# Value product of a windowed attention: from one 128-row product per unit to two 64-row products by halves of the keys

## The chip, the cores and the metric

The program runs on one core of a Trainium2 chip. The metric is device time in microseconds (us) of one execution, as the median of several runs. Engines are called PE (TensorE matmul), PEld (TensorE weight load), DVE (VectorE), ACT (ScalarE), POOL (GpSimd) and SP (SyncE, which only issues DMAs here).

## What is computed

A token-wise gate mixes an attention block and a gated linear unit over one sequence of 2048 tokens of width 512, all in float32:

```
g = sigmoid((x * gate_w).sum(-1, keepdims=True))
# a: 32 heads of width 16, causal, each query sees the last 256 keys
qkv = x @ wqkv
scores = einsum("bhqd,bhkd->bhqk", q, k) * 16 ** -0.5, masked to 0 <= i - j < 256
a = (softmax(scores) @ v) @ wo
# b: F = 1376
b = (sigmoid(x @ w_gate) * (x @ w_up)) @ w_down
out = g * a + (1 - g) * b
```

## The kernel before

**Stages.** A first stage (to about 38 us of the span) loads and splits x and the first weights and makes V and the first projections. Large products run in the reduced float32 type with each operand split into a high and a low part, so that a product over 512 inputs takes 12 matmuls (4 blocks of 128 inputs, 3 pairs of parts). The second stage, to about 560 us, is a loop over u (L766). The last stage makes the two output projections and the mix.

**Units.** The attention is cut into 128 units: 8 groups of 4 heads times 16 blocks of 128 tokens. Unit w needs three steps, which the loop does at different u: `s_part` (L305) at u = w makes the scores of a query block against its keys and DVE takes their maximum (L321); `st_part` (L353) at u = w + 9 (`LAG`) makes the scores again with keys on the rows and ACT takes the exponential into the tile `pt` (L366), which POOL masks (L368); the value product at u = w + 11 (`PVLAG`) multiplies `pt` (128 keys by up to 3 x 128 queries) with the values of 4 heads and adds to the PSUM tile `pv` (L394). A key block serves 3 query blocks (2 and 1 at the end of a group), 45 blocks of 128 columns in 16 units. `pv` is one bank of 4 query blocks used as a ring, so the product is cut in two where it wraps (6 of 16 units).

**Array halves.** The score matmuls have 64 rows: head hh uses rows 0 to 63 or 64 to 127 by hh % 2 (`blk`, L298). All work that fills the loop, the projections of queries and keys (`pj`), of the gated unit (`gu`) and its tail (`tp`), is also done with 64 rows at a time: `group_mm` (L242) takes half of the rows of a block. A generator `turns` (L632) hands this work out: one turn is one matmul of 512 columns on the lower half (half 0) and one on the upper (half 1), of different output tiles. Three groups of 12 steps go through each half in different orders (`TURN`), the upper half 6 turns behind (`SHIFT`), so that the second half of a group starts 6 turns after its first half ended and adds to the same PSUM tile. `turns` yields after 3 turns (`GAP`).

**Order of a unit.** PE, ACT, SP and DVE follow the order in which the loop is written. For u from 9 to 127 the loop does, for each of 4 heads, one `s` matmul on one half and one `st` matmul on the other, and then 3 turns (none after the last head of odd u), so 21 turns in two units. At the start of every even u it does the value products of two units as one burst: for each query range 4 matmuls of 128 rows by 32 columns, one for each head, beside each other in the array. After a burst `o_take` copies the two finished query blocks from `pv` (L410, ACT, 256 columns) and DVE clears them (L411). Copies out of PSUM at the end of a group wait in a list `acts` and are emitted one at each head; `behind` is the same for DVE. PSUM has two tiles each for `s` and `st`, three for `misc` (pj, gu, tp) and one for `pv`.

Of the kernel before, what the change touches and what calls it, by code (L numbers as in the profile page):

```python
# [10 lines left out]
AF = mybir.ActivationFunctionType  # L11
# [9 lines left out]
HG = 4  # L21
# [19 lines left out]
SD = 3  # L41
QB = 32
HOLD = 3
GAP = 3
SHIFT = 6
TURN = ((0, 2, 1), (1, 0, 2))
TAIL = 109
# [9 lines left out]
def gated_mix_kernel(  # L57
# [71 lines left out]
    with ExitStack() as actx:  # L129
# [112 lines left out]
        def group_mm(pt, wh, wl, c, k, half, second):  # L242
            d, w = divmod(k, 2) if k < 2 * ND else (k - 2 * ND, 2)
            r = slice(0, P) if half is None else slice(64 * half, 64 * half + 64)
            mm(pt, (wl if w == 2 else wh)[r, d], (xl if w == 1 else xh)[r, d, c * CH:(c + 1) * CH],  # L245
               start=k == 0 and not second, stop=k == 3 * ND - 1 and (half is None or second),
               skip_group_check=half is not None)

        def proj_mm(s, k, half=None, second=False):
            g, c = divmod(s, NC)  # L250
            if s not in pj:
                pj[s] = ps.tile([P, CH], F32, tag="misc", name=f"pj{s}", bufs=3)
            group_mm(pj[s], *wq[g], c, k, half, second)

        def proj_raw(s):
            raws[s] = cpool.tile([P, CH], F32, tag="sp", name=f"pr{s}", bufs=4)
# [48 lines left out]
        def s_part(u, hh):  # L305
            g, i = divmod(u, NB)
            s = g * NC + i // 4
            if i % 4 == 0 and hh == 0:
                mxs[s] = spool.tile([P, HG, 4], F32, tag="mx", name=f"mx{s}")
            k0 = max(0, i - 2)  # L310
            tag = "st" if u < LAG and hh >= 2 else "s"
            pt = ps.tile([P, 3 * P], F32, tag=tag, name=f"s{u}_{hh}", bufs=2)
            lhsT = blk(g, i, hh, 0)
            for k, e in pieces(g, k0, i + 1):
                mm(  # L315
                    pt[:, (k - k0) * P:(e - k0) * P], lhsT, blk(g, k, hh, 1, e - k),
                    start=k == k0, stop=e == i + 1, skip_group_check=True,
                )
            n = (i + 1 - k0) * P
            junk = spool.tile([P, 3 * P], F32, tag="junk", name=f"junk{u}_{hh}", bufs=1)  # L320
            nc.vector.tensor_tensor_reduce(  # L321
                junk[:, 0:n], pt[:, 0:n], mask[:, 3 * P - n:], scale=1.0, scalar=NEG,
                op0=ALU.add, op1=ALU.max, accum_out=mxs[s][:, hh, i % 4:i % 4 + 1],
            )
# [24 lines left out]
            )  # L349

        pts = {}

        def st_part(u, hh):  # L353
            g, j = divmod(u, NB)
            if u not in pts:
                pts[u] = ppool.tile([P, HG, 3 * P], F32, tag="pt", name=f"pt{u}", bufs=3)
            pt = ps.tile([P, 3 * P], F32, tag="st", name=f"st{u}_{hh}", bufs=2)
            lhsT = blk(g, j, hh, 1)
            last = min(NB, j + 3)
            for q, e in pieces(g, j, last):  # L360
                mm(  # L361
                    pt[:, (q - j) * P:(e - j) * P], lhsT, blk(g, q, hh, 0, e - q),
                    start=q == j, stop=e == last, skip_group_check=True,
                )
            n = (last - j) * P
            nc.scalar.activation(pts[u][:, hh, 0:n], pt[:, 0:n], AF.Exp, scale=SCALE)  # L366

        def mask_p(u):  # L368
            j = u % NB
# [12 lines left out]
        acts = []  # L382
        obs = {}

        def pv_part(u):
            g, j = divmod(u, NB)
            p = pts.pop(u)
            last = min(NB, j + 3)
            q = j
            while q < last:  # L390
                e = min(last, (q // 4 + 1) * 4)
                for hh in range(HG):
                    h = g * HG + hh
                    mm(  # L394
                        pv[32 * hh:32 * hh + 32, (q % 4) * P:(q % 4 + e - q) * P],
                        V[:, j, h * VW:h * VW + 32],
                        p[:, hh, (q - j) * P:(e - j) * P],
                        start=False, stop=True, skip_group_check=True,
                        tile_position=(0, 32 * hh),
                    )  # L400
# [4 lines left out]
        def o_take(s, half):  # L405
            g, c = divmod(s, NC)
# [3 lines left out]
            nc.scalar.copy(obs[s][:, cols], pv[:, cols])  # L410
            behind.insert(0, lambda: nc.vector.memset(pv[:, cols], 0.0))  # L411
            if half == 0:
# [79 lines left out]
        def gu_mm(f, c, w, k, half=None, second=False):  # L492
            if (f, c, w) not in gp:
                gp[f, c, w] = ps.tile([P, CH], F32, tag="misc", name=f"gu{f}_{c}_{w}", bufs=3)
            group_mm(gp[f, c, w], gv[:, 0, w], gv[:, 1, w], c, k, half, second)

        def gu_post(f, c, w):
            t = cpool.tile([P, CH], F32, tag="sp", name=f"sp{f}_{c}_{w}", bufs=4)
# [35 lines left out]
        def tail_mm(b, k, half=None, second=False):  # L534
            if b not in tp:
                tp[b] = ps.tile([P, CH], F32, tag="misc", name=f"tp{b}", bufs=3)
            d, w = divmod(k, 3)
            r = slice(0, P) if half is None else slice(64 * half, 64 * half + 64)
            mm(tp[b][:, 0:TW], (xl if w == 1 else xh)[r, d, b * P:(b + 1) * P], tw[d][int(w == 2)][r, 0:TW],  # L539
               start=k == 0 and not second, stop=k == 3 * ND - 1 and (half is None or second),  # L540
               skip_group_check=half is not None)

# [89 lines left out]
        def turns():  # L632
            k3 = 3 * ND
            groups = []
            halves_done = {}
            for t in range(n_rest * k3 + SHIFT):
                if t and t % GAP == 0:
                    yield
                if t % (3 * k3) == 0 and len(groups) < n_rest:
                    groups.extend((work or rest).pop(0) for _ in range(3))  # L640
                for half, v in enumerate((t, t - SHIFT)):
                    if 0 <= v < n_rest * k3:
                        n, k = divmod(v, k3)
                        n += TURN[half][n % 3] - n % 3
                        groups[n][0](k, half, n in halves_done)
                        if k == k3 - 1:
                            halves_done[n] = halves_done.get(n, 0) + 1
                            if halves_done[n] == 2:
                                _, after, post = groups[n]
                                if after is None:  # L650
                                    post()
                                else:
                                    acts.insert(0, lambda after=after, post=post: (post(), after()))

        def slot(h, d, c):
            return (xh, xl)[h][:, d, c * CH:(c + 1) * CH]
# [109 lines left out]
        for u in range(N):  # L766
# [42 lines left out]
            for hh in range(HG):  # L809
                if hh == 0 and u % 2 == 0:  # L810
                    for w in (u - PVLAG - 1, u - PVLAG):
                        if 0 <= w < NU:
                            pv_part(w)
                if u < NU:
                    s_part(u, hh)
                if 0 <= u - LAG < NU:
                    st_part(u - LAG, hh ^ 1 if u < NU else hh)
                if u < LAG:
# [5 lines left out]
                else:  # L824
                    if behind:
                        behind.pop(0)()
                    if acts and (u < NU or hh % 2 == 1):
                        acts.pop(0)()
                if u >= LAG and (hh < HG - 1 or u % 2 == 0 if u < NU else hh % 2 == 1):
                    next(slots, None)  # L830
                    if u >= NU and not (hh == HG - 1 and u % 2 == 1 and u > NU + 1):
                        next(slots, None)
            if u < LAG:
                flush(soon)
# [192 lines left out]
```

## Time and profile before

| | before |
|---|---|
| median of 3 runs | 738.04 us (737.7 to 738.16) |
| the profiled execution | 737.77 us |
| its span, first to last instruction | 736.1 us |
| granted TensorE clock over the span | 1.00 |
| PE busy | 730.0 us (99%) |
| DVE, ACT, POOL busy | 507.1 us, 430.4 us, 170.7 us |

The profile is that of one execution, so sums are made against 737.77 us, 1.7 us of which lie outside the span. Starts of matmuls are recorded and their ends are modelled, so that durations overlap: what an instruction takes is read from start to start. In a row of the timeline, "64\*128" after the tiles' names is the part of the array that a matmul uses, rows by columns; "64x384" is its moving operand, and "x4" merges neighbours of one kind into a row.

### The profile page before, as it was taken

The page shows a single profiled execution, that of the slowest core. Times are in us where ns is not written, and L with a number is a line of the kernel's source. Part 1 is how long each engine was busy: PE and PEld are TensorE (multiplying, and loading weights), DVE is VectorE, ACT ScalarE, POOL GpSimd, SP SyncE. Part 2 cuts the span into 40 slices and gives each one's busy share as a digit, 9 for nine tenths or more (in the row PEclk, how much of TensorE's full clock was granted, in tenths as well). Part 3 has the DMA queues.
Part 4 walks back from the last instruction along what each step waited for, and adds up shares of the span by engine and source line. Part 5 has one row for each costly group of instructions (what it writes and reads, how often), then busy time and mean ns, then how long its engine had stood idle before and what let it go on. Part 6 is the DMA issues. An engine that isn't in the chain of part 4 may idle for free.

```text
span 736.1 us, 17727 instructions
## 1 busy us (share of the span) xinstructions
PE 730.0 (99%) x6298; PEld 578.3 (79%) x6298; DVE 507.1 (69%) x1519; ACT 430.4 (58%) x922; POOL 170.7 (23%) x256
## 2 busy tenths in 40 slices
PE   9999999999999999999999999999999999999997
PEld 7888777887777878778777777778887888787886
DVE  5378867667776776776777677678846877658481
ACT  6423666576666666756757667676566654534341
POOL 5200333233233232323323323323341000000000
PEclk9999999999999999999999999999999999999999
DMA  8441334534445353452534524544477867878431
GB/s 300 108 116 43 102 106 120 152 88 127 129 116 142 86 153 109 123 156 59 165 106 107 152 76 128 160 135 152 154 233 190 281 173 175 224 172 252 131 74 57
DMA packets 94464, 103.65 MB, mean 141 GB/s; under 512 B 44942, under 2 KB 57486, under 8 KB 94376
## 3 DMA queue, kind: packets, MB, share of 16 engines
q1 hardware_dynamic: 94376, 102.53, 50.0%
q8 instruction: 49, 0.80, 0.5%
q14 instruction: 39, 0.32, 0.1%
HBM read 45.32 MB, written 31.99 MB: 105 GB/s over the span
## 4 chain that ended last, share of the span: by engine, by line
PE 97%; DVE 1%; DMA 1%; issue 1%; ACT 0%; SPq 0%; DVEq 0%
PE gu L245 28%; PE pv L394 12%; PE pj L245 11%; PE s L315 7%; PE st L361 5%; PE tp L539 5%; PE pd L79 5%; PE pd L81 5%; PE pd L80 5%; PE vh L576 3%; PE pa L79 2%; PE pa L80 2%; PE pa L81 2%; PE vps L440 1%; DVE junk L321 1%; DMA V<-in_wv_dram 1%
## 5 line engine op out<-in xcount | busy, mean ns | idle before, releaser
L321 DVE CUSTOM_DVE_ANT_0 junk<-s,mask 128x384 f32<-128x384 f32 (+2 forms) x512 | 271.6, 530 | 123.4 <-PE s L315 57.3
L366 ACT ACTIVATE pt<-st 128x384 f32<-128x384 f32 (+2 forms) x512 | 241.1, 475 | 166.0 <-PE st L361 66.6
L245 PE MATMUL gu<-xh,w 64*128 64x512 f32 x1152 | 271.1, 393 | 0.0
L245 PE MATMUL gu<-xl,w 64*128 64x512 f32 x576 | 183.0, 392 | 0.0
L371 POOL TENSOR_SCALAR_AFFINE_SELECT pt<-pt 128x512 f32<-128x512 f32 x128 | 86.5, 675 | 373.2 <-ACT pt L366 369.6
L361 PE MATMUL st<-ring 64*128 64x384 f32 (+2 forms) x536 | 168.1, 331 | 0.0
L315 PE MATMUL s<-ring 64*128 64x384 f32 (+2 forms) x536 | 166.7, 329 | 0.7 <-DVE mx L321 0.7
L245 PEld LDWEIGHTS gu<-xh,w 64*128 64x128 f32 x1152 | 150.9, 185 | 13.7
L315 PEld LDWEIGHTS s<-ring 64*128 64x128 f32 x536 | 95.3, 184 | 39.8 <-DVE nm L332 8.1
L361 PEld LDWEIGHTS st<-ring 64*128 64x128 f32 x536 | 96.3, 184 | 10.3 <-issue 2.7
L394 PE MATMUL pv<-pt,V 128*32 128x384 f32 (+2 forms) x1408 | 91.0, 388 | 0.0
L245 PEld LDWEIGHTS gu<-xl,w 64*128 64x128 f32 x576 | 87.7, 185 | 4.0
L245 PE MATMUL pj<-xl,wqh 64*128 64x512 f32 (+1 forms) x228 | 80.0, 392 | 0.0
L245 PE MATMUL pj<-xh,wqh 64*128 64x512 f32 (+1 forms) x228 | 79.8, 392 | 0.0
L376 POOL TENSOR_SCALAR_AFFINE_SELECT pt<-pt 128x512 f32<-128x512 f32 x112 | 74.8, 668 | 0.0
L245 PE MATMUL pj<-xh,wql 64*128 64x512 f32 (+1 forms) x228 | 69.8, 391 | 0.0
L394 PEld LDWEIGHTS pv<-pt,V 128*32 128x32 f32 x1408 | 37.2, 109 | 35.1 <-issue 28.8
L79 PE MATMUL pd<-ring,hb 128*128 128x512 f32 x160 | 63.1, 395 | 0.0
L81 PE MATMUL pd<-ring,hb 128*128 128x512 f32 x160 | 62.8, 393 | 0.0
L80 PE MATMUL pd<-ring,hb 128*128 128x512 f32 x160 | 62.1, 388 | 0.0
L75 ACT CAST hb<-V 128x512 fp32r<-128x512 f32 x40 | 24.9, 622 | 61.7 <-DVE V L730 47.7
L245 PEld LDWEIGHTS pj<-xh,wql 64*128 64x128 f32 (+1 forms) x228 | 41.2, 185 | 3.1
(129 smaller groups left out, 1133.1 us busy)
## 6 DMA issues: line engine op xcount, KB each, us to landing
gu_scratch<-sp SPq DMA_DIRECT2D x72, 256.0 KB
V<-gu_scratch SPq DMA_DIRECT2D x36, 512.0 KB
ring<-sh SPq DMA_DIRECT2D x128, 128.0 KB
ring<-sl SPq DMA_DIRECT2D x64, 128.0 KB
guraw<-in_wgu_dram SPq DMA_DIRECT2D x18, 256.0 KB
oT_scratch<-ob SPq DMA_DIRECT2D x128, 32.0 KB
xl<-oT_scratch SPq DMA_DIRECT2D x16, 256.0 KB
out_dram<-spare SPq DMA_DIRECT2D x16, 256.0 KB
```

What stands on the lines that cost most here:

```text
L79: mm(ps, lh, rh, start=first, stop=False)
L80: mm(ps, lh, rl, start=False, stop=False)
L81: mm(ps, ll, rh, start=False, stop=last)
L245: mm(pt, (wl if w == 2 else wh)[r, d], (xl if w == 1 else xh)[r, d, c * CH:(c + 1) * CH], start=k == 0 and not second, stop=k == 3 * ND - ...
L315: mm(pt[:, (k - k0) * P:(e - k0) * P], lhsT, blk(g, k, hh, 1, e - k), start=k == k0, stop=e == i + 1, skip_group_check=True,)
L321: nc.vector.tensor_tensor_reduce(junk[:, 0:n], pt[:, 0:n], mask[:, 3 * P - n:], scale=1.0, scalar=NEG, op0=ALU.add, op1=ALU.max, accum_out ...
L361: mm(pt[:, (q - j) * P:(e - j) * P], lhsT, blk(g, q, hh, 0, e - q), start=q == j, stop=e == last, skip_group_check=True,)
L366: nc.scalar.activation(pts[u][:, hh, 0:n], pt[:, 0:n], AF.Exp, scale=SCALE)
L371: nc.gpsimd.affine_select(p[:, :, 0:P], p[:, :, 0:P], pattern=[[0, HG], [1, P]], compare_op=ALU.is_ge, fill=0.0, base=0, channel_multiplie ...
L376: nc.gpsimd.affine_select(p[:, :, 2 * P:], p[:, :, 2 * P:], pattern=[[0, HG], [-1, P]], compare_op=ALU.is_gt, fill=0.0, base=0, channel_mu ...
L394: mm(pv[32 * hh:32 * hh + 32, (q % 4) * P:(q % 4 + e - q) * P], V[:, j, h * VW:h * VW + 32], p[:, hh, (q - j) * P:(e - j) * P], start=Fals ...
L539: mm(tp[b][:, 0:TW], (xl if w == 1 else xh)[r, d, b * P:(b + 1) * P], tw[d][int(w == 2)][r, 0:TW], start=k == 0 and not second, stop=k == ...
```

## The change

- The value product of a unit is divided by keys: `pv_quads(w, 0)` takes keys 0 to 63 on the lower half of the array and `pv_quads(w, 1)` keys 64 to 127 on the upper half, each with 4 matmuls of 64 rows by 32 columns for a query range. The last two units keep 128 rows.
- A unit has two bursts in place of four pairs. In burst 0 the value product on the lower half is written beside the four score matmuls (`s` and `st` of heads 1 and 3) of the upper half, in burst 1 the other way round. Where the product is cut in two, the second part is written after the first score matmul. Behind each burst stand 5 turns (6 behind burst 1 of odd u).
- Each unit's finished query block is copied and cleared by itself, 128 columns a unit, right after its second burst; the two value products of a unit follow each other by one burst, and the next unit's first product needs the cleared tile.
- Explicit dependencies (`after`): the first value matmul of each half waits for the last exponential emitted so far, and the first matmul of the second half of a group for the first exponential emitted after its first half.
- Copies at the end of a group are emitted in `turns` itself, not by way of `acts`.

```diff
-GAP = 3
+    def after(ins, other):
+        tc.add_manual_dep(
+            ins.ins, other.ins.name,
+            mybir.DependencyInfo(mybir.DependencyClass.Sync, mybir.DependencyReason.DATA), reason="array halves",
+        )
...
-            nc.scalar.activation(pts[u][:, hh, 0:n], pt[:, 0:n], AF.Exp, scale=SCALE)
+            exps.append(nc.scalar.activation(pts[u][:, hh, 0:n], pt[:, 0:n], AF.Exp, scale=SCALE))
...
-        def pv_part(u):
+        def pv_quads(u, half=None):
             g, j = divmod(u, NB)
-            p = pts.pop(u)
+            p = pts[u] if half == 0 else pts.pop(u)
             last = min(NB, j + 3)
-            q = j
-            while q < last:
-                e = min(last, (q // 4 + 1) * 4)
+            r = slice(0, P) if half is None else slice(64 * half, 64 * half + 64)
+
+            def quad(q, e):
                 for hh in range(HG):
                     h = g * HG + hh
-                    mm(
+                    ins = mm(
                         pv[32 * hh:32 * hh + 32, (q % 4) * P:(q % 4 + e - q) * P],
-                        V[:, j, h * VW:h * VW + 32],
-                        p[:, hh, (q - j) * P:(e - j) * P],
+                        V[r, j, h * VW:h * VW + 32],
+                        p[r, hh, (q - j) * P:(e - j) * P],
                         start=False, stop=True, skip_group_check=True,
-                        tile_position=(0, 32 * hh),
+                        tile_position=(r.start, 32 * hh),
                     )
-                q = e
-            if j % 2 == 1:
-                acts.insert(0, lambda: o_take(g * NC + j // 4, j // 2 % 2))
+                    if hh == 0 and q == j:
+                        after(ins, exps[-1])
+
+            cuts = [j, *range((j // 4 + 1) * 4, last, 4), last]
+            return [lambda q=q, e=e: quad(q, e) for q, e in zip(cuts, cuts[1:])]
...
-            cols = slice(2 * P * half, 2 * P * half + 2 * P)
+            cols = slice(k * P, (k + 1) * P)
             nc.scalar.copy(obs[s][:, cols], pv[:, cols])
             behind.insert(0, lambda: nc.vector.memset(pv[:, cols], 0.0))
-            if half == 0:
+            if k < 3:
                 return
...
             for t in range(n_rest * k3 + SHIFT):
-                if t and t % GAP == 0:
-                    yield
...
-                        groups[n][0](k, half, n in halves_done)
+                        ins = groups[n][0](k, half, n in halves_done)
+                        if k == 0 and n in halves_done:
+                            after(ins, exps[halves_done[n]])
                         if k == k3 - 1:
-                            halves_done[n] = halves_done.get(n, 0) + 1
-                            if halves_done[n] == 2:
-                                _, after, post = groups[n]
-                                if after is None:
-                                    post()
-                                else:
-                                    acts.insert(0, lambda after=after, post=post: (post(), after()))
+                            if n not in halves_done:
+                                halves_done[n] = len(exps)
+                            else:
+                                groups[n][2]()
+                                if groups[n][1]:
+                                    groups[n][1]()
+                yield
...
+            else:
+                w = u - PVLAG
+                for half in range(2):
+                    quads = []
+                    if 0 <= w < NU and (half == 0 or w < NU - 2):
+                        quads = pv_quads(w, half if w < NU - 2 else None)
+                    for hh in (1 - half, 3 - half):
+                        if quads:
+                            quads.pop(0)()
+                        if u < NU:
+                            s_part(u, hh)
+                        if quads:
+                            quads.pop(0)()
+                        if u - LAG < NU:
+                            st_part(u - LAG, hh)
+                    if 0 <= w < NU and half == 1:
+                        acts.insert(0, lambda w=w: o_take(w))
+                    for _ in range(2):
+                        if behind:
+                            behind.pop(0)()
+                        if acts:
+                            acts.pop(0)()
+                    for _ in range(5 + (half and u % 2)):
                         next(slots, None)
```

How the order on PE changes is shown at two places. In these rows "[waits ...]" names the engines whose semaphores the instruction waits for, `s_1` and `st_1` are the scores of head 1, the shapes give the array's full rows whatever the half, and "x3" merges the other three heads. The first place, before, is the burst of the value products of units 48 and 49, between two head pairs:

```order
L315 MATMUL s_3_4370<-ring 128x384 [waits DVE_49]
L361 MATMUL st_2_4374<-ring 128x384 [waits Activation_49]
L394 MATMUL pv<-pt_4197,V 32x384 [waits Pool_49]
L394 MATMUL pv<-pt_4197,V 32x384 x3
L394 MATMUL pv<-pt_4268,V 32x384 [waits Pool_49]
L394 MATMUL pv<-pt_4268,V 32x384 x3
L315 MATMUL s_0_4402<-ring 128x384 [waits DVE_49]
L361 MATMUL st_1_4407<-ring 128x384 [waits Activation_49]
L245 MATMUL pj_4236<-xh,wqh_3469 128x512
L245 MATMUL gu_2_1_4287<-xh,w_72 128x512
```

The same place in the changed kernel, burst 1 of unit 49, with the turn ahead of it and the first turn behind it:

```order
L250 MATMUL gu_3_1_4754<-xh,w_72 128x512 [waits Activation_49]
L250 MATMUL gu_2_1_4593<-xh,w_72 128x512
L400 MATMUL pv<-pt_4580,V 32x384 [waits Activation_49]
L400 MATMUL pv<-pt_4580,V 32x384 x3
L320 MATMUL s_0_4761<-ring 128x384 [waits DVE_49]
L367 MATMUL st_0_4765<-ring 128x384
L320 MATMUL s_2_4768<-ring 128x384 [waits DVE_49]
L367 MATMUL st_2_4772<-ring 128x384
L250 MATMUL gu_3_1_4754<-xl,w_72 128x512
L250 MATMUL gu_2_1_4593<-xl,w_72 128x512
```

The value matmuls of one unit's upper keys now stand directly ahead of four score matmuls of one half, where two units' products stood between two pairs; they wait for ACT, and so does the first matmul of a second group half in the turn ahead.

The second place is unit 50, whose query range wraps in the ring. Before, the burst of units 50 and 51:

```order
L394 MATMUL pv<-pt_4334,V 32x256 [waits Pool_49]
L394 MATMUL pv<-pt_4334,V 32x256 x3
L394 MATMUL pv<-pt_4334,V 32x128 [waits Pool_49]
L394 MATMUL pv<-pt_4334,V 32x128 x3
L394 MATMUL pv<-pt_4406,V 32x128 [waits Pool_49]
L394 MATMUL pv<-pt_4406,V 32x128 x3
L394 MATMUL pv<-pt_4406,V 32x256 [waits Pool_49]
L394 MATMUL pv<-pt_4406,V 32x256 x3
```

In the changed kernel, burst 0 of unit 50:

```order
L400 MATMUL pv<-pt_4650,V 32x256 [waits DVE_49,Pool_49]
L400 MATMUL pv<-pt_4650,V 32x256 x3
L320 MATMUL s_1_4799<-ring 128x384
L400 MATMUL pv<-pt_4650,V 32x128 [waits Pool_49]
L400 MATMUL pv<-pt_4650,V 32x128 x3
L367 MATMUL st_1_4808<-ring 128x384
L320 MATMUL s_3_4811<-ring 128x384
L367 MATMUL st_3_4815<-ring 128x384
```

A score matmul of the other half now stands between the two parts of the product, and the first value matmul of the unit waits for DVE as well, which clears the block of the unit before.

More of the change, by code (lines that the diff above doesn't have):

```diff
@@ L252, in proj_mm @@
                 pj[s] = ps.tile([P, CH], F32, tag="misc", name=f"pj{s}", bufs=3)
-            group_mm(pj[s], *wq[g], c, k, half, second)
+            return group_mm(pj[s], *wq[g], c, k, half, second)
         def proj_raw(s):
@@ L307, in s_part @@
             s = g * NC + i // 4
-            if i % 4 == 0 and hh == 0:
+            if s not in mxs:
                 mxs[s] = spool.tile([P, HG, 4], F32, tag="mx", name=f"mx{s}")
@@ L351, in gated_mix_kernel @@
         pts = {}
+        exps = []
         def st_part(u, hh):
@@ L494, in gu_mm @@
                 gp[f, c, w] = ps.tile([P, CH], F32, tag="misc", name=f"gu{f}_{c}_{w}", bufs=3)
-            group_mm(gp[f, c, w], gv[:, 0, w], gv[:, 1, w], c, k, half, second)
+            return group_mm(gp[f, c, w], gv[:, 0, w], gv[:, 1, w], c, k, half, second)
         def gu_post(f, c, w):
@@ L808, in gated_mix_kernel @@
                 hold_group(*rest.pop(0))
[L809 to L814, printed above, removed]
+            if u < LAG:
+                for hh in range(HG):
                     s_part(u, hh)
-                if 0 <= u - LAG < NU:
-                    st_part(u - LAG, hh ^ 1 if u < NU else hh)
-                if u < LAG:
                     flush(behind)
```

20 lines of the change are left out of this document (7 added, 13 removed).

## The prediction

> **What bounds the kernel now.** I read the page first, for the engine that sets the end, then who waits for whom, then one stretch of the second stage row by row. From the page, the busy times, the first line of the chain that ended last and its lines:
>
> ```profile
> PE 730.0 (99%) x6298; PEld 578.3 (79%) x6298; DVE 507.1 (69%) x1519; ACT 430.4 (58%) x922; POOL 170.7 (23%) x256
> PE 97%; DVE 1%; DMA 1%; issue 1%; ACT 0%; SPq 0%; DVEq 0%
> ```
>
> PE is on the chain for 97% of the span. The waits of PE, from the view of waits:
>
> ```profile
> PE warm_ps L185 <- DVE warm L180: 1.2, 1, 1.2
> PE s L315 <- DVE mx L321: 0.7, 2, 0.4
> ```
>
> So in the loop PE waited 0.7 us for anybody. A gain must come from PE's own time, and a loss from that or from a new wait. To price PE's time I need units. In the groups of the window from 96.47 to 469.65 us:
>
> ```profile
> L321 DVE DVE_READ_ACCUMULATOR2_ANT mx<- 128x1 f32 x384 | 31.9, 83 | 0.0
> L394 PEld LDWEIGHTS pv<-pt,V 128*32 128x32 f32 x1056 | 27.9, 109 | 26.3 <-issue 21.7
> ```
>
> 384 maxima are 96 units of 4 heads, so a unit takes 373.18 / 96 = 3.89 us. The 1056 weight loads are 11 a unit; the program has 22 products of 4 heads in 16 units, 5.5 a unit, so each value matmul runs as two passes.
>
> Now the matmul starts in such a unit (start, length, then what; the rows of 64\*128 are halves that run beside each other):
>
> ```profile
> 401.30 0.39 PE L245 MATMUL gu<-xh,w 64*128 64x512 f32 x2
> 401.53 0.33 PE L315 MATMUL s<-ring 64*128 64x384 f32 x1
> 401.54 0.33 PE L361 MATMUL st<-ring 64*128 64x384 f32 x1
> 401.71 0.39 PE L245 MATMUL gu<-xh,w 64*128 64x512 f32 x1
> 401.71 0.39 PE L245 MATMUL gu<-xl,w 64*128 64x512 f32 x1
> 401.94 0.62 PE L245 MATMUL gu<-xh,w 64*128 64x512 f32 x3
> 402.18 0.39 PE L245 MATMUL gu<-xl,w 64*128 64x512 f32 x1
> 402.40 0.33 PE L361 MATMUL st<-ring 64*128 64x384 f32 x1
> 402.41 0.33 PE L315 MATMUL s<-ring 64*128 64x384 f32 x1
> ```
>
> A pair of scores costs 401.71 - 401.53, some 0.17 us with rounding, 3 turns cost 402.40 - 401.71 = 0.69, so a turn is 0.23. The weights of the scores are loaded while the turn before them streams, as the load rows of the same stretch show:
>
> ```profile
> 401.30 0.18 PEld L315 LDWEIGHTS s<-ring 64*128 64x128 f32 x1
> 401.31 0.18 PEld L361 LDWEIGHTS st<-ring 64*128 64x128 f32 x1
> ```
>
> Now a burst of value products of two units, matmuls and then loads:
>
> ```profile
> 405.88 0.33 PE L361 MATMUL st<-ring 64*128 64x384 f32 x1
> 405.89 0.33 PE L315 MATMUL s<-ring 64*128 64x384 f32 x1
> 406.15 1.50 PE L394 MATMUL pv<-pt,V 128*32 128x384 f32 x16
> 407.58 0.32 PE L315 MATMUL s<-ring 64*128 64x128 f32 x1
> ...
> 406.15 0.16 PEld L394 LDWEIGHTS pv<-pt,V 128*32 128x32 f32 x8 [0.31 <-issue]
> 406.50 0.13 PEld L394 LDWEIGHTS pv<-pt,V 128*32 128x32 f32 x4 [0.19 <-issue]
> 406.82 0.13 PEld L394 LDWEIGHTS pv<-pt,V 128*32 128x32 f32 x4 [0.19 <-issue]
> 407.58 0.18 PEld L315 LDWEIGHTS s<-ring 64*128 64x128 f32 x1 [0.62 <-DVE nm L331]
> ```
>
> Passes follow each other by 406.82 - 406.50 = 0.32 us at 384 columns, and the 16 matmuls are four passes: 4 heads run beside each other. Going in costs 406.15 - 405.88 = 0.27 in place of 0.17, so 0.10 more; the burst takes 1.43 for 4 x 0.32 = 1.28, so 0.15 more. **A visit to the other form of the array costs 0.25 us.** On both sides the weights come no earlier than the matmul: the overlap seen at 401.30 is gone. The sum holds: two units are 7 x (0.17 + 0.69) + 0.17 + 0.10 + 1.43 = 7.72, measured 2 x 3.89 = 7.78.
>
> **The question of the change.** Array time by itself is equal before and after: a half has four scores, one pass pair over its half of the keys and 10.5 turns in a unit either way. All depends on whether a 64\*32 value matmul on one half runs beside 64\*128 scores on the other. No row of this profile has two forms at once. Two facts bear on it. First, the wait at a change of form isn't special to the value product. At the first scores of the loop, after 128\*128 projections:
>
> ```profile
> 37.91 0.39 PE L245 MATMUL pj<-xh,wql 128*128 128x512 f32 x1
> 38.23 0.33 PE L315 MATMUL s<-ring 64*128 64x128 f32 x2
> ...
> 38.23 0.18 PEld L315 LDWEIGHTS s<-ring 64*128 64x128 f32 x2 [0.35 <-issue]
> ```
>
> A matmul of 512 columns is followed after 0.32 here, where 0.23 is the rule, again 0.09 more and again without an early load. Rows against columns, in or out: every change of form empties the array by about 0.1 us, although an early load as such is possible. That looks like one setting for the whole array. Second, in one form the halves are free of each other:
>
> ```profile
> 127.69 0.38 PE L315 MATMUL s<-ring 64*128 64x256 f32 x1
> 127.69 0.33 PE L361 MATMUL st<-ring 64*128 64x128 f32 x1
> ...
> 127.91 0.22 PE L315 MATMUL s<-ring 64*128 64x128 f32 x1
> ```
>
> In the program the two `s` pieces come first and `st` third, but `st` starts on its half while the second `s` waits for its own.
>
> I take the one setting: then 64\*32 and 64\*128 can't overlap, and each burst is value product first, scores after it. The Trainium skill, TensorEngine Tiling (Array Packing), Tiling Modes, lists 64×128 and 64×32 as separate configurations of the array and says that "Changing tiling mode (not just tile) drains the TensorE". By this rule the sum is the one below; were the rule confined to tiles that share rows, it would be that of the first or second rival. No run so far shows a half in one mode beside a half in another.
>
> **The sum**, for the 117 units with all steps (u = 11 to 127), each against before:
>
> - *Value product twice.* 45 blocks in 16 units are 360 columns a unit: two passes of 360/384 x 0.32 = 0.30 make 0.60 us. Before, all 128 keys took that; now each half takes it, one after the other: +0.60.
> - *Scores in a row.* Four scores at 0.17 x 360/384 = 0.16 stand on one half. The other half goes ahead with its turns meanwhile, but the next burst's value product is for the half behind and needs the array's form, so the lead is lost there. 8 x 0.16 in place of 4 pairs: +0.64.
> - *Visits.* One in two units before, 0.125 a unit. Now two a unit, and one more in each burst of the 6 in 16 units where the product is cut around a score: 2.75 x 0.25 = 0.69, so +0.56.
>
> That is 1.80 us a unit, 117 x 1.80 = 211 us. For u = 128 to 136 only `st` remains: +0.60, scores 4 x 0.16 for 2 x 0.16, +0.32, visits 2 x 0.25 - 0.125, +0.38: 1.30 x 9 = 12 us. The last two units keep their form. The sum is +223 us: 737.8 + 223 = 961; the profiled 737.77 stands 0.3 us under the median, which I neglect. I take **960 us**.
>
> *Costed at nothing*, with the cover named. Turns are equal in number. DMAs are the same and SP's order is kept. The copies of `pv` are cut in two, and ends of groups are emitted elsewhere. Both go to engines with room; in 16 units (PE, PEld, DVE, ACT, POOL busy):
>
> ```profile
> 96.47:158.80 62.33, 62.33 (x658) 48.85 (x654) 44.40 (x156) 41.02 (x93) 20.48 (x31) 1.00 0.45 124
> ```
>
> ACT is free for 21 of 62 us, DVE for 18. *The new waits* stop PE's queue, so all turns behind them. The tight one is the next unit's value product, which needs exponentials, copy and clearing behind burst 1:
>
> ```profile
> 401.94 0.51 ACT L366 ACTIVATE pt<-st 128x384 f32<-128x384 f32 x1
> 402.32 0.62 ACT L153 CAST wqh<-wqraw 128x512 fp32r<-128x512 f32 x1
> ...
> L410 ACT COPY ob<-pv 128x256 f32<-128x256 f32 x48 | 17.7, 368 | 0.0
> L411 DVE MEMSET pv<- 128x256 f32 x48 | 13.1, 272 | 2.5
> ```
>
> The exponential starts 0.40 after its score (401.54), and ACT's next 0.38 later. In the forecast the burst's last score starts 0.25 + 0.60 + 3 x 0.16 = 1.33 after the last turn's stream, copy 2.11, done by 2.48, cleared by 2.75 (these lengths are for 256 columns, so upper ones). The next value product is due at 0.25 + 0.60 + 0.64 + 5 x 0.23 = 2.64, or 2.87 with 6 turns. So nothing, or 0.11 in every second unit, 6 us. If one copy of a group more (0.62, the cast above) stands ahead on ACT in every second unit, 0.3 x 117 = 35 us. Below nothing it can't be, since before had no such wait. I take nothing and keep 35 as the upper end.
>
> *Its own range*: if the new visits cost nothing at all, 0.60 + 0.64 - 0.125 = 1.12 a unit and 0.80 in the nine: 138 us, so 876; above, 961 + 35, about 1000.
>
> **The rivals.** *Each half has its own form, without a drain.* Then a half does what it did before without its 0.125 a unit: 126 x 0.125 = 16 us less, 722. Against it stands the wait above: last score at about 0.50, copy 1.28, cleared by 1.92, due at 0.66 + 5 x 0.23 = 1.81: up to 0.11 in every second unit, 6 us, and up to 35 with copies ahead as above. So 722 to 757; I take 727, nearest to the chain without extra copies. For it: the freedom at 127.69. Against: the lost early load in every change of form. This is the faster side.
>
> *Each half has its own form and drains alone.* Then a half pays one visit of 0.25 a unit in place of 0.125: +16 us, and the wait of up to 0.11 at half the units, 6: 754 to 760, up to 789 with copies ahead. It decides when the drain is a matter of the half's own rows.
>
> *Starts in strict order.* Forms overlap, but a matmul may not start before its predecessors: the scores then start when the second pass does, 0.32 late in each burst, 2 x 0.32 x 117 = 75 us on 738 - 16, near 800. The row at 127.69 speaks against it. The Trainium skill, TensorE: Matmul & The Clock Gate, Part 3, What overlaps and what doesn't, says that matmuls start in program order without exception; here `st` starts 0.22 us before the second `s` that precedes it, so the trace differs and decides.
>
> **How the numbers follow.** Forecast (one form for the array) 0.66; own form with drain 0.15; own form without 0.15; strict order 0.04. About 0.2%, 1.5 us, is what a measurement of this kernel can tell from no change. Only the free rival comes near or under that line: of its 0.15, 0.11 faster, 0.03 within and 0.01 slower, so faster 0.11, same 0.03, slower 0.86. The forecast's own range, 876 to 1000, may hold nine tenths of its 0.66, since three terms lean on one price; with 0.15 and 0.04 that is 0.78. So the range reaches into the free rival too: 725 to 1000.
>
> **What would show it.** Right: in a burst the scores start after the last value pass of the other half, about 0.4 us behind it as at 407.58, their weights not loaded early; one half's turns begin with the scores of the other; 16 units take 91 us, not 62; PE's waits stay a few us. Wrong: scores within some ns of the value product's first pass. Then the clock of the unit tells the rivals apart: 3.77 us without, 4.0 with drain; and if PE waits for DVE at the value product by tens of us, the clearing took the place.

## The result and the profile after

The changed kernel takes 1000.92 us (median of 4 runs, 1000.46 to 1000.99) beside 737.87 us for the kernel before in the same comparison: 1.356 times the time (95% interval 1.3548 to 1.358). The direction and the mechanism were as forecast, 960 us was 41 us short, and the time lies 0.9 us above the range.

The page of the changed kernel, busy times and the chain that ended last:

```profile
PE 988.7 (99%) x7690; PEld 664.2 (67%) x7690; DVE 517.5 (52%) x1583; ACT 426.2 (43%) x986; POOL 162.5 (16%) x256
PE 97%; issue 1%; DVE 1%; ACT 1%; POOL 0%; ACTq 0%; DVEq 0%; POOLq 0%
```

PE is still the chain, and DVE and ACT work about as long as before. The view of waits shows what PE waited for in the loop:

```profile
PE pv L400 <- DVE pv L421: 1.9, 5, 0.9
PE tp L549 <- ACT pt L372: 0.3, 1, 0.3
PE s L320 <- DVE mx L326: 0.3, 1, 0.3
```

This view counts only the time in which all of PE is idle. The starts say the same: an undisturbed value product follows the last turn by 0.31 to 0.32 us, and over the whole loop the products come 3.3 us later than that in sum. So the new dependencies cost next to nothing here. Units, from the groups of the window from 151 to 724 us:

```profile
L326 DVE DVE_READ_ACCUMULATOR2_ANT mx<- 128x1 f32 x384 | 31.7, 83 | 0.0
L400 PEld LDWEIGHTS pv<-pt,V 64*32 64x32 f32 x2112 | 41.9, 104 | 83.5 <-issue 64.2 <-POOL pt L377 5.7 <-POOL pt L382 5.5
```

384 maxima are 96 units in 573 us, 5.97 us a unit for 3.89 before, and value weights are loaded 22 times a unit for 11. One burst of a whole product in the timeline of PE; to the left the start, and the "x8" row holds both passes of four heads:

```profile
517.69 0.39 PE L250 MATMUL gu<-xh,w 64*128 64x512 f32 x1
518.00 0.85 PE L400 MATMUL pv<-pt,V 64*32 64x384 f32 x8
518.78 0.44 PE L320 MATMUL s<-ring 64*128 64x384 f32 x1
519.06 0.33 PE L367 MATMUL st<-ring 64*128 64x384 f32 x1
519.07 0.49 PE L250 MATMUL gu<-xl,w 64*128 64x512 f32 x1
519.24 0.33 PE L320 MATMUL s<-ring 64*128 64x384 f32 x1
519.41 0.33 PE L367 MATMUL st<-ring 64*128 64x384 f32 x1
```

And the loads of the first two scores in the timeline of the same burst:

```profile
518.78 0.18 PEld L320 LDWEIGHTS s<-ring 64*128 64x128 f32 x1 [0.62 <-issue]
518.89 0.19 PEld L367 LDWEIGHTS st<-ring 64*128 64x128 f32 x1
```

The scores stand directly behind the value product in the program and use the other half, yet the first starts 0.78 us after it, behind both passes (2 x 0.32), and its weights aren't loaded a moment earlier. Then the two halves run beside each other again: the turn of 519.07 belongs to the half that had the value product, while the other has three more scores to do. Half by half, the forecast's picture holds. What it had wrong can be read here too: 519.06 - 518.78 is 0.28 us for a score that costs 0.17 (519.41 - 519.24).

### The profile page after: what moved, and what is told of

The parts are those of the page before. It is cut to its first block, busy times and chain, and to the rows that moved or that the text cites. A ratio compares the mean times of both kernels' runs of the same rounds, so it can differ in the third digit from the quotient of the medians.

```text
span 998.8 us, 20800 instructions
## 1 busy us (share of the span) xinstructions
PE 988.7 (99%) x7690; PEld 664.2 (67%) x7690; DVE 517.5 (52%) x1583; ACT 426.2 (43%) x986; POOL 162.5 (16%) x256
## 4 chain that ended last, share of the span: by engine, by line
PE 97%; issue 1%; DVE 1%; ACT 1%; POOL 0%; ACTq 0%; DVEq 0%; POOLq 0%
PE gu L250 24%; PE pv L400 20%; PE s L320 10%; PE pj L250 9%; PE st L367 7%; PE tp L549 4%; PE pd L84 4%; PE pd L86 4%; PE pd L85 4%; PE vh L586 3%; PE pa L84 2%; PE pa L86 1%; PE pa L85 1%; PE vps L450 1%; ACT pt L372 1%
## 5 line engine op out<-in xcount | busy, mean ns | idle before, releaser
L372 ACT ACTIVATE pt<-st 128x384 f32<-128x384 f32 (+2 forms) x512 | 215.2, 469 | 419.0 <-PE st L367 392.4
L250 PE MATMUL gu<-xh,w 64*128 64x512 f32 x1152 | 311.2, 404 | 1.0
L400 PE MATMUL pv<-pt,V 64*32 64x384 f32 (+2 forms) x2800 | 224.7, 392 | 3.4 <-DVE pv L421 1.9
L250 PE MATMUL gu<-xl,w 64*128 64x512 f32 x576 | 214.8, 405 | 0.0
L250 PEld LDWEIGHTS gu<-xh,w 64*128 64x128 f32 x1152 | 178.8, 184 | 17.4 <-ACT pt L372 7.7
L377 POOL TENSOR_SCALAR_AFFINE_SELECT pt<-pt 128x512 f32<-128x512 f32 x128 | 81.9, 640 | 642.0 <-ACT pt L372 636.0
L320 PE MATMUL s<-ring 64*128 64x384 f32 (+2 forms) x536 | 185.1, 366 | 0.4 <-DVE mx L326 0.3
L400 PEld LDWEIGHTS pv<-pt,V 64*32 64x32 f32 x2800 | 56.5, 105 | 110.1 <-issue 82.4
L250 PEld LDWEIGHTS gu<-xl,w 64*128 64x128 f32 x576 | 99.1, 184 | 5.2
L382 POOL TENSOR_SCALAR_AFFINE_SELECT pt<-pt 128x512 f32<-128x512 f32 x112 | 71.3, 637 | 0.0
L509 ACT COPY sp<-gu 128x512 f32<-128x512 f32 x72 | 43.0, 597 | 8.2 <-PE gu L250 7.7
```

The costliest lines, as they stand in the source:

```text
L250: return mm(pt, (wl if w == 2 else wh)[r, d], (xl if w == 1 else xh)[r, d, c * CH:(c + 1) * CH], start=k == 0 and not second, stop=k == 3 ...
L320: mm(pt[:, (k - k0) * P:(e - k0) * P], lhsT, blk(g, k, hh, 1, e - k), start=k == k0, stop=e == i + 1, skip_group_check=True,)
L372: exps.append(nc.scalar.activation(pts[u][:, hh, 0:n], pt[:, 0:n], AF.Exp, scale=SCALE))
L377: nc.gpsimd.affine_select(p[:, :, 0:P], p[:, :, 0:P], pattern=[[0, HG], [1, P]], compare_op=ALU.is_ge, fill=0.0, base=0, channel_multiplie ...
L382: nc.gpsimd.affine_select(p[:, :, 2 * P:], p[:, :, 2 * P:], pattern=[[0, HG], [-1, P]], compare_op=ALU.is_gt, fill=0.0, base=0, channel_mu ...
L400: ins = mm(pv[32 * hh:32 * hh + 32, (q % 4) * P:(q % 4 + e - q) * P], V[r, j, h * VW:h * VW + 32], p[r, hh, (q - j) * P:(e - j) * P], star ...
```

## The experiments

The theory: the array has one form at a time; value products and scores take turns, and each change of form has a price. Rivals: the loss is made by the new waits and the order of the queue, by float32 passes on 64 rows, or by scores in a row on one half. A time without an interval is that of a single run.

**Value products in the form of the scores.** The edit, with three of the four heads' value products left out and other columns of V taken:

```diff
-                for hh in range(HG):
+                for hh in range(1):
...
-                        pv[32 * hh:32 * hh + 32, (q % 4) * P:(q % 4 + e - q) * P],
-                        V[r, j, h * VW:h * VW + 32],
+                        pv[:, (q % 4) * P:(q % 4 + e - q) * P],
+                        V[r, j, 0:P],
...
-                        tile_position=(r.start, 32 * hh),
```

> The changed kernel with its value matmuls of 64 rows by 128 columns, the form of the scores: one matmul for each query range and key half in place of four, with the same columns and the same two passes. It leaves out the value products of three of the four heads and takes other columns of V, so only its time is read. One form for the whole array (theory): nothing has to change form any more, so the value product runs beside the scores of the other half; a unit needs 3.89 us less the 0.125 to 0.19 that it paid for visits before, some 3.70 to 3.80, and the time is 715 to 735 us. Rival, that the new waits and the order of the queue make the loss, or the float32 passes on 64 rows: these are kept, so the time stays near 1000 us.

Measured: 827.08 us, ratio to before 1.1206 (1.119 to 1.1223). 174 of the 263 us are gone, and the overlap is there. The burst's starts in the timeline of this run:

```profile
401.06 0.39 PE L250 MATMUL pj<-xh,wqh 64*128 64x512 f32 x1
401.57 0.34 PE L399 MATMUL pv<-pt,V 64*128 64x128 f32 x1
401.58 0.44 PE L320 MATMUL s<-ring 64*128 64x384 f32 x1
```

Value product and score start 0.01 us apart. But 827 isn't 735, so with the form out of the way something else holds PE. The longest of its waits, 28.5 us in all:

```profile
PE pv L399 <- DVE pv L419: 28.5, 68, 1.2
```

And the clearing ahead of this burst in the timeline of DVE:

```profile
401.26 0.17 DVE L419 MEMSET pv<- 128x128 f32 x1
```

The clearing ends at 401.43 and the product starts at 401.57, 0.51 us after the last turn's start in place of 0.23: the wait that the prediction had put into its free rival at 0.11 us.

**Control: one value matmul in place of four, in the old form.** Three heads are left out as well, and the tile is cleared to one:

```diff
-                for hh in range(HG):
+                for hh in range(1):
...
-            behind.insert(0, lambda: nc.vector.memset(pv[:, cols], 0.0))
+            behind.insert(0, lambda: nc.vector.memset(pv[:, cols], 1.0))
```

> Control to the run with 64 by 128 columns: also one value matmul in place of four, but left in the form of 64 rows by 32 columns. It leaves out the value products of three of the four heads and clears their tile to one, so only its time is read. One form for the whole array: visits, passes and scores in a row are as in the changed kernel, so 990 to 1001 us. Rival, that the number of value matmuls or of column tiles makes the loss: the time falls with the number of matmuls, to well under 900 us.

Measured: 993.63 us. The number of matmuls and of column tiles in use is worth 7 us. The two runs differ in the columns of the matmul, 32 or 128, and so in the form: 167 us lie between them.

**Loosened waits, form of the scores.** Built on the first run, with the same parts left out:

```diff
-                        after(ins, exps[-1])
+                        after(ins, exps[-2])
...
-            if k == 0:
+            if k % 2 == 0:
+                return
+            if k == 1:
...
-            cols = slice(k * P, (k + 1) * P)
+            cols = slice((k - 1) * P, (k + 1) * P)
```

> The run with value matmuls of 64 by 128 columns (827.1 us) with its two waits loosened and the form kept: the second half of a value product waits for the last exponential but one, and the tile is copied and cleared every second unit, 256 columns as before the change. Leaves out three of four heads' value products as that run did. If the 92 us between that run and the 735 us expected of it are these waits, in its trace each value product starts 0.05 us behind an exponential or 0.12 us behind a clearing, the time falls most of the way: 740 to 780 us. Rival, that float32 passes on 64 rows cost more beside scores: it stays above 810 us.

Measured: 798.78 us. A miss: 28 us gained where 47 to 87 were expected, above the theory's 780 and under the rival's 810. Its waits show why that was too little:

```profile
PE pv L399 <- DVE pv L421: 21.2, 46, 1.4
PE pv L399 <- POOL pt L377: 7.5, 16, 0.7
```

PE still waits for the clearing, and longer than in the first run (3.9 us) for the mask on POOL. So the copy and the clearing of the tile were taken out of the loop altogether:

```diff
-            nc.scalar.copy(obs[s][:, cols], pv[:, cols])
-            behind.insert(0, lambda: nc.vector.memset(pv[:, cols], 0.0))
+            nc.scalar.copy(obs[s][:, cols], V[:, j, 0:2 * P])
```

> The run with value matmuls of 64 by 128 columns and loosened waits (798.8 us), with the value tile neither copied nor cleared: the copy reads V in its place, of the same size. It leaves out the use of the value product and three of four heads' products; only its time is read. One form for the whole array: the value product is wholly beside the scores, and no visit is left: 738 less 63 visits of 0.36 us, 23 us, is 715 us, up to 735 with the waits on the mask and on exponentials that stay. Rival, that float32 passes on 64 rows beside scores cost by themselves: 770 us or more.

Measured: 752.15 us, again a miss, by 17 us, but the rival's 770 isn't reached either. A burst of this run:

```profile
400.66 0.40 PE L250 MATMUL gu<-xl,w 64*128 64x512 f32 x1
400.80 0.39 PE L250 MATMUL pj<-xl,wqh 64*128 64x512 f32 x1
400.89 0.34 PE L320 MATMUL s<-ring 64*128 64x384 f32 x1
401.03 0.48 PE L399 MATMUL pv<-pt,V 64*128 64x384 f32 x1
401.07 0.33 PE L367 MATMUL st<-ring 64*128 64x384 f32 x1
401.27 0.44 PE L320 MATMUL s<-ring 64*128 64x384 f32 x1
401.35 0.48 PE L399 MATMUL pv<-pt,V 64*128 64x384 f32 x1
```

The value product follows its turn by 0.23 us, the step of a turn, so a float32 matmul enters behind reduced ones and beside a score with no loss. The second pass comes 0.32 later, as ever. 249 of the 263 us come back with form and waits removed, though some 7 of them belong to the value matmuls left out, as the control showed; what holds the last 14 above before, and 17 above what was expected, isn't settled.

**Parts of a cut product together.**

```diff
-                        if quads:
+                        while quads:
                             quads.pop(0)()
                         if u < NU:
                             s_part(u, hh)
-                        if quads:
-                            quads.pop(0)()
```

> The changed kernel with the two parts of a cut value product written one behind the other, no score between them. That takes away one visit in 88 bursts (44 units among those with scores that are cut, two bursts each). One form for the whole array: 88 x 0.25 us, the price of the prediction, gives 979 us; at the 0.37 us that a burst of the changed kernel costs over its passes and scores it is 968 us. Rival, that the second part runs beside the scores anyway: no change, 1001 us.

Measured: 974.11 us, ratio to before 1.3206 (1.3184 to 1.3228). 26.8 us for 88 visits is 0.30 us each, between the two figures. The rival falls.

**Scores in pairs on both halves.**

```diff
-                    for hh in (1 - half, 3 - half):
+                    for hh in (half, half + 2) if u < NU else (1 - half, 3 - half):
...
-                            st_part(u - LAG, hh)
+                            st_part(u - LAG, hh ^ 1 if u < NU else hh)
```

> The changed kernel with the scores of each burst in pairs on both halves as before (s of one head beside st of its neighbour), the value products by halves kept. One form for the whole array: the scores then cost two pairs in a burst, not four in a row, 4 x 0.16 us a unit less, 117 x 0.64 = 75 us: about 926 us. Rival, that each half has its own form: a half's work is the same and its scores now stand behind its own value product, so the time stays near 1000 us.

Measured: 965.29 us, 36 us less, half of what was expected. In a cut burst the second part of the product stands between a pair's two scores and tears it, which the expectation had overlooked, and the value product waits for the clearing (12.4 us). So both edits were made at once:

> Both earlier edits at once: scores in pairs on both halves, and the parts of a cut value product together, so that no pair is torn by a second visit. Measured 974.1 us with the parts together alone. One form for the whole array: 4 x 0.16 us a unit less for 117 units, 75 us: about 899 us, up to 12 more for waits on the clearing of the value tile, as the run with pairs alone showed (12.4 us). Rival, that scores in pairs are worth only the 36 us that the run with pairs alone gained: about 938 us.

Measured: 927.74 us, 46 us under the run with the parts together; the expectation was 63 to 75 and the rival's figure 938. With shorter bursts the clearing comes late again. The waits of this run:

```profile
PE pv L400 <- DVE pv L421: 16.9, 48, 1.2
```

These 16.9 us are only the time in which no matmul runs at all, and the run with the parts together had 3.6 of them. From the starts, counted as for the changed kernel, the value products come 25.8 us late here and 4.9 there. Without these 21 us more, scores in pairs are worth 67 of the 75 us; the other 8 stay open.

**The value product whole, the two bursts kept.** All 128 rows in burst 0, nothing in burst 1:

```diff
-                    if 0 <= w < NU and (half == 0 or w < NU - 2):
-                        quads = pv_quads(w, half if w < NU - 2 else None)
+                    if 0 <= w < NU and half == 0:
+                        quads = pv_quads(w)
```

> The changed kernel with the value product whole again: all 128 rows in burst 0, none in burst 1, everything else kept, the scores of a burst on one half too. One form for the whole array: one value product a unit in place of two (0.60 us less), one visit in place of 2.75, and the lead that one half wins in burst 0 is used in burst 1, where nothing changes form, so the scores cost as in pairs: before plus one visit in place of half a visit a unit, 126 x 0.5 x 0.25 to 0.40 us, 754 to 763 us. Rival, that scores in a row on one half cost by themselves, whether or not a change of form stands between the bursts: 0.64 us a unit more, near 835 us.

Measured: 864.14 us, a plain miss of 100 us, and above the rival's figure too. The expectation had left out the second visit of the cut products, one in each of 44 units. Another part is the clearing, still behind burst 1. In the waits of this run:

```profile
PE pv L400 <- DVE pv L421: 28.5, 58, 1.7
```

One clearing in the timeline of DVE:

```profile
403.21 0.17 DVE L421 MEMSET pv<- 128x128 f32 x1
```

And the value product behind it in that of PE, with the idle time before it and what ended that:

```profile
403.52 0.32 PE L400 MATMUL pv<-pt,V 128*32 128x128 f32 x4 [0.68 <-DVE pv L421]
```

With the copy and the clearing put right behind burst 0, and cut parts together:

```diff
-                    if 0 <= w < NU and half == 1:
+                    if 0 <= w < NU and half == 0:
                         acts.insert(0, lambda w=w: o_take(w))
```

> The run with the value product whole in burst 0 (864.1 us), with its cut parts together and the tile copied and cleared right behind burst 0, so that the next value product, two bursts later, no longer stands close behind the clearing. One form for the whole array, with a visit of 0.36 us as the bursts of the kernel before cost when the first scores behind them are counted in (0.10 + 0.15 + 0.11): 126 half visits more than before, 23 us, about 761 us; up to 770 with waits left. Rival, that four scores in a row on one half cost 0.64 us a unit even with no change of form between the bursts: near 836 us.

Measured: 814.94 us, 54 us over the theory's 761 and 21 under the rival's 836. Neither figure fits, so the rows had to say. In a unit of this run, DVE:

```profile
411.59 1.02 DVE L276 TENSOR_TENSOR sl<-pr,sh 128x512 fp32r<-128x512 f32 x1
412.53 0.54 DVE L326 CUSTOM_DVE_ANT_0 junk<-s,mask 128x384 f32<-128x384 f32 x1
413.23 0.56 DVE L326 CUSTOM_DVE_ANT_0 junk<-s,mask 128x384 f32<-128x384 f32 x1
413.71 0.08 DVE L326 DVE_READ_ACCUMULATOR2_ANT mx<- 128x1 f32 x1
```

The matmuls of PE in the same unit, and two of their weight loads:

```profile
413.43 0.34 PE L367 MATMUL st<-ring 64*128 64x384 f32 x1
413.66 0.39 PE L250 MATMUL gu<-xh,w 64*128 64x512 f32 x1
413.85 0.45 PE L320 MATMUL s<-ring 64*128 64x384 f32 x1
413.89 0.47 PE L250 MATMUL gu<-xl,w 64*128 64x512 f32 x1
...
413.85 0.18 PEld L320 LDWEIGHTS s<-ring 64*128 64x128 f32 x1 [0.24 <-DVE mx L326]
413.86 0.18 PEld L250 LDWEIGHTS gu<-xl,w 64*128 64x128 f32 x1
```

The second `s` of burst 1 needs a score tile that DVE only gives back at 413.79. It starts 0.42 us behind the `st` before it where 0.17 is the rule, while the other half keeps its step (413.66 and 413.89). With one burst's scores close together, two score tiles don't reach. So here it isn't only the row of scores itself, but its demand on DVE. From 60 to 760 us the trace has 78 units whose scores all have 384 columns. In 52 of them this score is late, and each time a maximum ended less than 0.15 us before it. On average this step is 0.12 us too long, and the 54 us are 0.43 a unit: a part, then, and the rest was not tried by itself.

**Twice the visits, before.** The kernel before with one unit in every burst:

```diff
-                if hh == 0 and u % 2 == 0:
-                    for w in (u - PVLAG - 1, u - PVLAG):
-                        if 0 <= w < NU:
-                            pv_part(w)
+                if hh == 0 and 0 <= u - PVLAG < NU:
+                    pv_part(u - PVLAG)
```

> The kernel before with the value product of one unit in every unit's burst, in place of two units in every second one; nothing else is changed. That doubles the visits of the value product: 63 more over the loop. With the prediction's price of 0.25 us for a visit 738.0 + 15.8 = 754 us; with 0.36 us, the weights of the first scores behind a visit counted in, 738.0 + 22.7 = 761 us. Rival, that the scores or the waits behind a burst hide a part of the visit: below 750 us.

Measured: 763.51 us, ratio 1.0348 (1.0331 to 1.0365). 25.6 us for 64 further bursts are **0.40 us a visit**; 0.25 falls. The waits of this run in the loop:

```profile
PE s L315 <- DVE mx L321: 2.0, 5, 0.4
PE pv L394 <- DVE pv L411: 0.9, 1, 0.9
```

That is 2.9 us for 0.7 before. Without these 2.2 us a visit costs 0.37 us, which fits the 0.36 of the expectation.

**Turns behind a visit, before.** The burst written behind the pair of the first head:

```diff
-                if hh == 0 and u % 2 == 0:
-                    for w in (u - PVLAG - 1, u - PVLAG):
-                        if 0 <= w < NU:
-                            pv_part(w)
                 if u < NU:
                     s_part(u, hh)
...
+                if hh == 0 and u % 2 == 0:
+                    for w in (u - PVLAG - 1, u - PVLAG):
+                        if 0 <= w < NU:
+                            pv_part(w)
```

> The kernel before with its burst of value products written behind the pair of the first head, not ahead of it, so that behind a visit come turns of 512 columns and not scores. Behind a visit the second weight load isn't early and shows 0.28 us after the first start; a matmul of 512 columns covers 0.21 to 0.23 of that, one of 384 columns 0.17. If so, each of 64 visits gains 0.05 us: 3 us, 735 us. Rival: exponentials of that pair come late behind the burst and PE waits for them later: the same or slower, 738 to 745 us.

Measured: 747.97 us, ratio 1.0132 (1.0115 to 1.0149). The idea was wrong. Behind the burst, in this run:

```profile
406.27 0.49 PE L245 MATMUL gu<-xl,w 64*128 64x512 f32 x1
406.27 0.73 PE L245 MATMUL gu<-xh,w 64*128 64x512 f32 x3
```

The last of these three starts at 0.73 - 0.39 = 0.34 us behind the first, counting 0.39 for its length as in the rows of turns: 0.11 over the 0.23 of a turn, as the first score paid 0.11 over 0.17. So the excess doesn't shrink with a wider matmul. It is as long as the step from the first load behind a visit to the second, 518.78 to 518.89 in the changed kernel; that the one makes the other is likely but not shown. Why the whole is 10 us slower wasn't followed further; its waits for maxima are 3.2 us for 0.7 before.

## Why the prediction was right in kind and short in size

- *One form for the whole array*: right. Scores start behind the last value pass (518.78), no load is early, and with matmuls of one form the overlap appears at once (401.57 and 401.58). The control excludes the number of matmuls, and the run without copy and clearing, float32 as before, excludes the float32 passes. Shown is this for 64 by 32 beside 64 by 128 alone.
- *Value product twice, +0.60*: right. There are twice as many passes (2112 loads for 1056), and a burst of two takes 0.78 us, 2 x 0.32 and 0.14 on the way out, where before four passes had 0.15.
- *Scores in a row, +0.64*: about right. The other half starts its turns while the row still runs (519.07). The runs in pairs gained 46 and 36 us of the 75 us that the row should be worth, 67 once the later value products are counted out.
- *Visits at 0.25 us*: this is the step that failed, a term of the sum that was too small. A unit of 5.97 us, less 1.20 for passes, 10.5 x 0.23 = 2.42 for turns and 8 x 0.16 = 1.28 for scores, leaves 1.07 us. That is 2.75 visits of 0.39 us, and the run with twice the visits measured 0.40, or 0.37 without its waits. The price was read as 0.10 on the way in and 0.15 on the way out, and the first pair behind the burst was taken at 0.17 like any other. It isn't; the trace of before shows it in an ordinary burst:

```profile
399.70 0.44 PE L315 MATMUL s<-ring 64*128 64x384 f32 x1
399.71 0.44 PE L361 MATMUL st<-ring 64*128 64x384 f32 x1
399.99 0.39 PE L245 MATMUL gu<-xl,w 64*128 64x512 f32 x1
```

0.28 us, 0.11 more. The burst that was quoted in the prediction had a first score of 128 columns and its turns merged into one row, where this doesn't show, and the check of the sum, 7.72 against 7.78, was let pass with just the kind of gap that it was made to find. With 0.36 the term is 2.25 x 0.36 = 0.81 for 0.56; the unit +2.05, 117 x 2.05 = 240, the nine units 0.60 + 0.32 + 0.54 = 1.46 each, 13: 738 + 253 = 991 us. So the visit explains 30 of the missing 41 us. With 0.40 the same sum gives 1002 us for 1000.9 measured, but that close a fit is partly luck, since 0.40 holds waits that the changed kernel mostly hasn't, and the second visits in cut bursts measured only 0.30. The trace tells where some of the rest lies: over passes, scores and turns, uncut bursts whose scores all have 384 columns cost 0.37 us, and those with scores of 128 columns 0.46 to 0.59. Why narrow scores cost more stays open.
- *The upper end*: 35 us for waits were added to 961, and nothing for the price of a visit, which had a lower end (nothing) and no upper one. The waits stayed small (1.9 us of idle PE), and the visit used up the room.
- *The tight chain through copy and clearing*: nearly hidden in the changed kernel, whose long bursts give it time, and a bound in the runs that shorten them and keep it behind burst 1 (28.5 us of bare waits with the form of the scores). The rival without drain was priced with 0.11 us at every second unit; the run nearest to it took 827 us, and its value product followed the last turn by 0.51 in place of 0.23. So even if the forms had overlapped, the kernel would probably not have been faster; no run shows 64\*32 matmuls overlapping with scores.

## What to carry to other kernels

Before work is put on different parts of the array at the same time, ask whether the parts have one form. If they haven't, as 64 by 32 and 64 by 128 here, expect them to take turns, at the price of a visit there and back, counted up to the second matmul behind it. When a price is used many times, check it on a stretch that differs only in the number of such events, take out the waits that this stretch adds, and treat a small gap in the check of a sum as a missing term. A schedule that packs producers closely also needs tiles and consumers that keep up: here a clearing and two score tiles came up as waits as soon as the change of form cost less.

## What the runs showed of the hardware that was not expected

The first matmul behind a change of form costs 0.11 us more whether it has 384 columns (0.28 for 0.17) or 512 (0.34 for 0.23). A float32 matmul of two passes enters beside and behind reduced-precision ones of the same form without a gap (401.03 - 400.80 = 0.23). And the view of waits counts only the time in which the whole engine is idle: a score that comes 0.25 us late on one half (413.85) beside a turn on the other (413.89) shows in the starts and the loads, and not in that total.
